# Attention and a four-expert MoE on one core: a small tile padded to 128 bytes, and three operand forms per pair of units written later

## Chip, cores and metric

One core of one Trainium2 chip. The metric is device time in microseconds (us), lower is better. The kernel before takes 1182.71 us, the median of three runs (1180.28 to 1183.48).

## The reference

The kernel computes attention with a local window and a few global keys, and feeds its output to four experts that are all applied to every token and mixed with given weights:

```python
def _attn_ref(q, k, v, n_global, n_local):     # 4 x 8 heads x 768 tokens x 64
    scores = scale * np.matmul(q, k.transpose(0, 1, 3, 2))
    ...
    scores = np.where(keep, scores + bias, -1000000000.0)
    ...
    return np.matmul(a, v).astype(np.float32)

def _moe_ref(x, domain_probs, w1, w2):         # x 3072 x 512, E = 4, F = 1024
    p = domain_probs / (domain_probs.sum(-1, keepdims=True) + 1e-09)
    for e in range(E):
        h = np.maximum(x @ w1[e], 0.0)
        out += p[:, e:e + 1] * (h @ w2[e])
    return out.astype(np.float32)
```

## The kernel before, in words

**Precision and fast multiplication.** Nearly all products of the experts run in fp32r. An operand is split into a high part (a rounded copy) and a low part (the operand less its high part), and three products, high by high, low by high and high by low, are summed in PSUM. Such a pair of parts is called a form here. The first matmul of an expert, x by w1, is a Strassen-Winograd product: x is cut into the blocks B11, B12, B21, B22 and their sums T1 to T4, w1 into A11, A12, A22 and sums S1 to S4, and seven block products (`product`, L850, 6 matmuls of 384 columns each) take the place of eight.

**Batches 0 and 1.** The attention of the first batch comes first (to about 63 us of the profile), then the expert layer of batches 0 and 1 with the attention of the later batches woven in. A unit is a batch, an expert and a group of 256 of the expert's 1024 inner columns: 16 units per batch. `first` (L872) makes the unit's hidden block and writes it, rectified, as tile `h` (pool `hp`, L1319); `second` (L937) multiplies it by w2: per unit 36 matmuls, `pm<-w2s,h`, with a piece of `h` of 128 x 128 as the stationary operand and 512 columns of `w2s` moving. Over the two batches these are 1152.

**Where the tiles lie.** Pools stand one behind the other in each partition of SBUF. Pool `fast` (L1275) holds the attention biases and `psumm` (L281), the 24 sums of the mixing weights, 96 bytes. It begins at a multiple of 64 bytes and ends, as built, at byte 130400, which is 32 past one. All pools opened behind it while it is open begin there or at whole multiples of 64 from it: the raw weights, the tiles of the attention (loaded q, k and v, their turned and split copies, the probabilities) and `h`. The forms of x, `w1s` and `w2s` lie ahead of it at multiples of 64. `early.close()` drops all of that; the pools of the turned batches (L1373) start afresh at a multiple of 64.

**Batches 2 and 3, the turned batches** (`turned_batch`, L982). Here the second matmul is a Strassen-Winograd product too. Two units make a pair j, eight pairs a batch. `small` (L1073) makes one unit's hidden block from seven products and leaves its four blocks, rectified and weighted, in the tiles hb["B11"], hb["B12"], hb["B21"] and hb["B22"], the even unit in the first half of each tile and the odd unit in the second. Once a pair has its blocks, `sums` (L995) makes T3, T1, T2 and T4 of them, and `form` (L988) writes the forms: ScalarE (ACT) the high part, a CAST, VectorE (DVE) or GpSimd (POOL) the low part, a subtraction. In the pair after it, `more` (L1183) calls `big` (L1049) seven times, between the products of `small`: n = 0 to 6 are A11 by B11, A12 by B21, S4 by B22, S3 by T3, S2 by T2, S1 by T1 and A22 by T4, of 12 matmuls each, `pq<-form,w2s` or `pq<-form,w2f`. n = 0 to 2 fall in the even unit, the rest in the odd one. A big product is added to an accumulator in SBUF by DVE; in the pair j = 1, where the accumulators are first written, ACT copies it there. The last pair of a batch is multiplied without turning (`multiply`, `pm<-w2s,form`: 12 matmuls of 512 columns per tile of 128 tokens, 144 in all), and the accumulators are turned back.

**What sets the order.** Each engine works through its own list. From the seventh step of batch 0 on a scheduler, at build time, sets the order on each engine, except that the instructions passed to `keep_in_program_order` keep theirs among each other and against what stands before them. The chain inside a unit: the matmuls of S2 by T2, S3 by T3 and A22 by T4 go on in the same accumulator (`pa`) as A11 by B11, and each has to wait until ACT has copied out what stood there: `u` (after S2 by T2) before S3 by T3 may start, `vv` (after S3 by T3) before A22 by T4. S4 by B22 goes on in the accumulator of S1 by T1 and waits until DVE has read that for block B22.

Names in the rows: hB_8000, hB_8001, hB_8002 and hB_8003 are hb["B11"], hb["B12"], hb["B21"] and hb["B22"]; hT_8004 is hb["T3"]; sumB_8005, sumB_8006 and sumB_8007 are the accumulators of big products 0, 1 and 2; `p`, `u` and `vv` are a unit's partial sums.

Of the kernel before, what the change touches and what calls it, by code (L numbers as in the profile page):

```python
# [9 lines left out]
F32 = mybir.dt.float32  # L10
# [8 lines left out]
P = 128  # L19
# [6 lines left out]
def f32(ap):  # L26
    return ap.bitcast(F32)
# [159 lines left out]
def attn_moe_kernel(ctx: ExitStack, tc, q, k, v, n_global, n_local, domain_probs, w1, w2, out):  # L187
# [19 lines left out]
    ve, ac, po, sy, te = (Ordered(tc, e) for e in (nc.vector, nc.scalar, nc.gpsimd, nc.sync, nc.tensor))  # L207
# [54 lines left out]
    NT = N // P  # L262
# [14 lines left out]
    def mixture():  # L277

        sy.dma_start(prob, domain_probs.rearrange("(t p) e -> p t e", p=P))
        yield  # L280
        psumm = fast.tile([P, NT, 1], F32, name="psumm")  # L281
        ve.reduce_sum(psumm, prob, axis=AX.X)
        ve.tensor_scalar_add(psumm, psumm, 1e-9)
        ve.reciprocal(psumm, psumm)
        for e in range(E):
            ve.tensor_mul(prob[:, :, e : e + 1], prob[:, :, e : e + 1], psumm)
# [485 lines left out]
    kept, waiting = {}, {}  # L772
# [209 lines left out]
    def turned_batch(b, L, hb, acc, raw):  # L982
# [2 lines left out]

        keeping = tc.keep_in_program_order

        def form(name, src, low):  # L988
            t = made[name] = L.form.tile([P, 2, 2, HALF], F32R, name="form")
            ac.copy(t[:, 0], src)  # L990
            ins = low.tensor_tensor(t[:, 1], src, f32(t[:, 0]), op=ALU.subtract)
            if low is po:
                keeping(ins)

        def sums():  # L995
            t3 = hb["T3"]
            ve.tensor_sub(t3, hb["B22"], hb["B12"])
            form("T3", t3, ve)
            ve.tensor_sub(hb["B12"], hb["B12"], hb["B11"])
            ve.tensor_add(hb["B11"], t3, hb["B11"])  # L1000
            form("T2", hb["B11"], ve)
            form("T1", hb["B12"], ve)
            ve.tensor_sub(hb["B21"], hb["B21"], hb["B11"])

        ORDER2 = (("A11", "B11"), ("A12", "B21"), ("S4", "B22"), ("S3", "T3"), ("S2", "T2"), ("S1", "T1"), ("A22", "T4"))

# [19 lines left out]
        def ask(j, n):  # L1026

            if j >= per // 2 - 1 or n in (0, 5):
                return
            e, g = divmod(j, NPR // 2)  # L1030
            names = {1: ("A11", "A12"), 2: ("S4",), 3: ("S3",), 4: ("S2",), 6: ("S1", "A22")}[n]
            if len(names) == 2:
                t = wp.tile([P, 2, 2, 2, 2 * P], F32R, name="w2s")
            else:
                t = L.w2f.tile([P, 1, 2, 2, 2 * P], F32R, name="w2f")
            for at, a in enumerate(names):
                to = w2f[(j, a)] = t[:, at]
                if a in value:
                    keeping(po.tensor_copy(to[:, :, 0], value[a]))
                    keeping(po.tensor_tensor(to[:, :, 1], value[a], f32(to[:, :, 0]), op=ALU.subtract))  # L1040
                else:
                    f, m = {"A11": (0, 0), "A12": (1, 0), "A22": (1, 1)}[a]
                    for u in range(2):
                        block = kept[(e, 2 * g + u, 2)][:, :, f, m * 2 * P : (m + 1) * 2 * P]
                        sy.dma_start(f32(to[:, u]), f32(block))
            if n == 6:
                ask_raw(j + 1)

        def big(j, n):  # L1049
            a, x = ORDER2[n]  # L1050
            pm = L.pq.tile([P, 2, 512], F32, name="pq")
            w, t = w2f[(j, a)], made[x]
            for m in range(2):
                at = 0
                for u in range(2):
                    for wi, xi in ((0, 0), (1, 0), (0, 1)):
                        te.matmul(
                            pm[:, m, :HALF], w[:, u, wi, m * P : (m + 1) * P], t[:, xi, u, :],
                            start=(at == 0), stop=(at == 5),
                        )  # L1060
                        at += 1
            if j == 0:
                ac.copy(acc[x], pm[:, :, :HALF])
            else:
                ve.tensor_add(acc[x], pm[:, :, :HALF], acc[x])
            if n == 0:
                form("T4", hb["B21"], ve)
            if j == per // 2 - 2:
                for to, other in {1: (("B21", "B11"),), 4: (("T2", "B11"), ("T3", "T2"))}.get(n, ()):
                    ve.tensor_add(acc[to], acc[to], acc[other])  # L1070
            ask(j + 1, n)

        def small(i, more, plain=None):  # L1073

            u = i % 2

            def out(name, f, c, src):
                if plain is None:
                    ve.scalar_tensor_tensor(
                        hb[name][:, u], src, 0.0, share[i][:, c * HALF : (c + 1) * HALF], op0=ALU.max, op1=ALU.mult  # L1080
                    )
                else:
                    if not plain:
                        for n in ((1, 0), (0, 1))[u]:
                            plain[n] = L.form.tile([P, 2, 2, HALF], F32R, name="form")
                    h = plain[f]
                    ac.activation(h[:, 0, c], src, AF.Relu)
                    ve.scalar_tensor_tensor(h[:, 1, c], src, 0.0, f32(h[:, 0, c]), op0=ALU.max, op1=ALU.subtract)
# [65 lines left out]
            h22 = hb["B22"][:, u]  # L1154
            ve.tensor_add(h22, pc[:, :HALF], u3)
            out("B22", 1, 1, h22)
            if u == 1 and plain is None:
                form("B22", hb["B22"], po)
            more()
# [13 lines left out]
        for j in range(per // 2):  # L1173
# [9 lines left out]
            def more():  # L1183
                if j > 0:
                    big(j - 1, at[0])
                else:
                    ask(0, at[0])
                at[0] += 1
# [6 lines left out]
            for i in (b * per + 2 * j, b * per + 2 * j + 1):  # L1195
                share[i] = pb
                plain = None
                if j == per // 2 - 1:
                    plain = final[i] = {}
                chores.append(load_w1(i + 2))  # L1200
                if j == per // 2 - 1:
                    chores.append(load_w2(i))
                for _ in small(i, more, plain):
                    work_chores()
                    yield
            if j < per // 2 - 1:
                sums()
# [67 lines left out]
    fast = early.enter_context(tc.tile_pool(name="fast", bufs=1))  # L1275
# [5 lines left out]
    with ExitStack() as start_stack:  # L1281
# [4 lines left out]
        for d, _ in enumerate(first_attention(A, bank)):  # L1286
# [19 lines left out]
            if d == 13:  # L1306
# [8 lines left out]
                last_forms(1, take, A)  # L1315
            work_chores()
        mix = mixture()
        next(mix)
    hp = early.enter_context(tc.tile_pool(name="hp", bufs=2))  # L1319
# [54 lines left out]
    hb = {n: L.hb.tile([P, 2, HALF], F32, name=f"h{n}") for n in ("B11", "B12", "B21", "B22", "T3")}  # L1374
# [39 lines left out]
```

## Time and profile before

| | us |
|---|---|
| median of three runs | 1182.71 |
| the profiled execution, whole | 1183.57 |
| its span, first to last instruction | 1181.8 |
| PE busy | 1155.9 (98%) |
| DVE busy | 841.2 (71%) |
| ACT busy | 527.8 (45%) |
| POOL busy | 469.0 (40%) |

The profiled execution is 0.86 us above the median, and 1.77 us of it lie outside the span. The busy time of PE counts a matmul up to its modelled end, so matmuls that follow each other overlap; how fast they follow is read from the starts in the timeline. PEld is the load of the stationary operand, which runs beside the matmul before it. An idle time is put down to what ended it.

### The profile page before, as it was taken

What the parts mean: (1) busy time and instruction counts of PE and PEld (TensorE: products, weight loads), DVE (VectorE), ACT (ScalarE), POOL (GpSimd) and SP (SyncE); (2) the same over time, 40 slices, a digit from 0 to 9 for tenths busy, and PEclk for the clock granted to TensorE, in tenths of its full rate; (3) what the DMA queues carried; (4) which work ended last, traced back from release to release, by engine and by line L of the source; (5) the groups of instructions that cost most, each with busy time, mean ns of one, the idle gap of its engine ahead of it and who ended that gap; (6) DMA issues with size and microseconds to landing.
All of it is one profiled execution on the core that took longest, in us unless ns stands there. A gap on an engine that the chain in (4) does not pass through costs nothing.

```text
span 1181.8 us, 19019 instructions
## 1 busy us (share of the span) xinstructions
PE 1155.9 (98%) x7101; PEld 1059.6 (90%) x7101; DVE 841.2 (71%) x1655; ACT 527.8 (45%) x1302; POOL 469.0 (40%) x437
## 2 busy tenths in 40 slices
PE   8989999999999999999999999999999999999998
PEld 6778888888888988888888899999999889999996
DVE  5976666676667766766666785787879566777784
ACT  5846666664655555445444314232234243222231
POOL 5666454545411000000000257666662376666620
PEclk9999999999999999999999999999999999999999
DMA  9578787767686675665655664666766556665532
GB/s 188 145 226 286 234 283 228 255 215 252 224 243 201 216 218 166 204 195 173 195 183 205 236 232 157 230 218 233 269 210 247 214 208 227 214 227 214 214 116 92
DMA packets 170116, 250.98 MB, mean 212 GB/s; under 512 B 108480, under 2 KB 144416, under 8 KB 157216
## 3 DMA queue, kind: packets, MB, share of 16 engines
q1 hardware_dynamic: 164976, 233.43, 60.7%
q0 software_dynamic: 4032, 14.68, 3.2%
q10 hardware_dynamic: 1008, 1.57, 0.4%
q8 instruction: 58, 0.95, 0.3%
q14 instruction: 42, 0.34, 0.1%
HBM read 194.04 MB, written 55.62 MB: 211 GB/s over the span
## 4 chain that ended last, share of the span: by engine, by line
PE 87%; DVE 8%; issue 1%; ACT 1%; DMA 1%; SPq 1%; POOL 0%; ACTq 0%; DVEq 0%
PE pm L42 62%; PE pq L42 14%; PE pt L42 7%; PE ps L42 4%; DVE hB L42 2%; DVE form L42 2%; DVE sumT L42 1%; DVE hT L42 1%; ACT form L42 1%; DVE pm L42 1%; SPq L42 1%; DVE sumB L42 0%; DMA first_k<-in_k_dram 0%; DMA raw<-in_moe_w_dram 0%; DMA raw_n<-in_n_local_dram 0%
## 5 line engine op out<-in xcount | busy, mean ns | idle before, releaser
L42 PE MATMUL pm<-xT,w1s 128*128 128x384 f32 x1536 | 303.8, 337 | 7.3 <-ACT vv L42 3.7
L42 PE MATMUL pm<-w2s,h 128*128 128x512 f32 x1152 | 286.2, 400 | 2.7 <-DVE h L42 2.7
L42 PEld LDWEIGHTS pm<-xT,w1s 128*128 128x128 f32 x1536 | 267.4, 188 | 10.5 <-ACT vv L42 4.4
L42 PEld LDWEIGHTS pm<-w2s,h 128*128 128x128 f32 x1152 | 212.6, 188 | 50.4 <-DVE h L42 3.5
L42 PE MATMUL pm<-xB,w1s 128*128 128x384 f32 x1152 | 229.4, 341 | 0.9 <-DVE hB L42 0.4
L42 PEld LDWEIGHTS pm<-xB,w1s 128*128 128x128 f32 x1152 | 203.5, 190 | 6.3 <-DVE hB L42 3.5
L42 DVE SCALAR_TENSOR_TENSOR acc<-pm,prob,acc 128x512 f32<-128x512 f32 x180 | 134.3, 749 | 75.8 <-PE pm L42 75.2
L42 POOL TENSOR_TENSOR xT<-x,xT 128x768 fp32r<-128x768 f32 x4 | 8.1, 2036 | 317.5 <-ACT xT L42 317.5
L42 PE MATMUL pq<-form,w2s 128*128 128x384 f32 x672 | 125.8, 334 | 0.0
L42 POOL TENSOR_TENSOR raw<-raw 128x512 f32<-128x512 f32 x56 | 74.7, 1334 | 113.8 <-DMA raw<-in_moe_w_dram 110.5
L42 PEld LDWEIGHTS pq<-form,w2s 128*128 128x128 f32 x672 | 117.3, 188 | 0.0
L42 ACT ACTIVATE pb<-pb,nmax 128x256 f32<-128x256 f32 (+1 forms) x192 | 92.5, 483 | 36.4 <-DVE nmax L42 35.7
L42 ACT CAST form<-hB 128x768 fp32r<-128x768 f32 x84 | 68.5, 836 | 85.5 <-DVE hB L42 85.5
L42 ACT COPY p<-pm 128x384 f32<-128x384 f32 x64 | 30.5, 477 | 147.9 <-PE pm L42 147.7
L42 PE MATMUL pq<-form,w2f 128*128 128x384 f32 x504 | 94.1, 334 | 0.0
L42 PEld LDWEIGHTS pq<-form,w2f 128*128 128x128 f32 x504 | 88.0, 188 | 0.0
L42 ACT ACTIVATE h<-pm 128x384 fp32r<-128x384 f32 x128 | 62.0, 488 | 54.2 <-DVE pm L42 49.7
L42 POOL TENSOR_TENSOR w2s<-raw,w2s 128x512 fp32r<-128x512 f32 x46 | 60.3, 1323 | 45.2 <-ACT w2s L42 43.9
L42 DVE SCALAR_TENSOR_TENSOR h<-pm,h 128x384 fp32r<-128x384 f32 x128 | 70.4, 552 | 7.7 <-ACT h L42 5.6
L42 DVE CUSTOM_DVE_ANT_0 pb<-ps,nbias 128x256 f32<-128x256 f32 (+1 forms) x144 | 50.3, 398 | 33.9 <-PE ps L42 27.7
L42 DVE TENSOR_TENSOR sumT<-pq,sumT 128x768 f32<-128x768 f32 x48 | 45.8, 953 | 36.9 <-PE pq L42 36.5
L42 ACT ACTIVATE pb<-pb,zsum 128x256 f32<-128x256 f32 (+1 forms) x144 | 62.5, 483 | 8.7 <-DVE zsum L42 8.3
(148 smaller groups left out, 1667.9 us busy)
## 6 DMA issues: line engine op xcount, KB each, us to landing
w1s<-kept SPq DMA_DIRECT2D x48, 1792.0 KB, 8.0
kept<-w1s SPq DMA_DIRECT2D x16, 1792.0 KB, 7.7
w2s<-kept SPq DMA_DIRECT2D x84, 256.0 KB, 5.0
w2s<-kept SPq DMA_DIRECT2D x20, 1024.0 KB, 4.9
raw<-in_moe_w_dram SPq DMA_DIRECT2D x32, 512.0 KB, 4.2
kept<-w2s SPq DMA_DIRECT2D x16, 1024.0 KB, 6.4
raw<-in_moe_w_dram POOLq DMA_DIRECT2D x28, 512.0 KB, 9.6
v<-in_v_dram SPq DMA_DIRECT2D x12, 384.0 KB, 5.8
```

The lines of the kernel that those rows point to most:

```text
L42: ins = fn(*args, **kwargs)
```

## The change

The sums of the mixing weights get a tile of 32 columns of which 24 are used, so that pool `fast` ends at byte 130432, a multiple of 64, and all that stands behind it moves up by 32 bytes: `h` from byte 142688 to 142720, for one. No tile of the turned batches moves.

In the turned batches T2 is added into T3's tile (once T3's form is made) and not into B11's. The forms of T2, T1 and T4 are no longer made in `sums` and at the first big product, but by a new function `rest_of_sums`, called in the even unit of the next pair behind the output of block B22. The three CASTs on ACT are kept in program order. The numbers of instructions on all engines stay the same.

```diff
-        psumm = fast.tile([P, NT, 1], F32, name="psumm")
+        psumm = fast.tile([P, 32, 1], F32, name="psumm")[:, :NT]
...
-        def form(name, src, low):
+        def form(name, src, low, kept=False):
             t = made[name] = L.form.tile([P, 2, 2, HALF], F32R, name="form")
-            ac.copy(t[:, 0], src)
+            ins = ac.copy(t[:, 0], src)
+            if kept:
+                keeping(ins)
             ins = low.tensor_tensor(t[:, 1], src, f32(t[:, 0]), op=ALU.subtract)
...
             form("T3", t3, ve)
             ve.tensor_sub(hb["B12"], hb["B12"], hb["B11"])
-            ve.tensor_add(hb["B11"], t3, hb["B11"])
-            form("T2", hb["B11"], ve)
-            form("T1", hb["B12"], ve)
-            ve.tensor_sub(hb["B21"], hb["B21"], hb["B11"])
+            ve.tensor_add(t3, t3, hb["B11"])
+            ve.tensor_sub(hb["B21"], hb["B21"], t3)
+
+        def rest_of_sums():
+            for name, src in (("T2", "T3"), ("T1", "B12"), ("T4", "B21")):
+                form(name, hb[src], ve, True)
...
-            if n == 0:
-                form("T4", hb["B21"], ve)
...
             out("B22", 1, 1, h22)
+            if u == 0:
+                rest_of_sums()
```

How this moves the instructions on ACT, in the pair j = 1 of batch 2 (the CASTs are the high parts of the forms, `u` and `vv` the copies that S3 by T3 and A22 by T4 wait for):

```order
 L42 CAST form<-hT_8004 128x768
 L42 COPY sumB_8005<-pq 128x768
 L42 COPY u<-pm 128x384
-L42 CAST form<-hB_8000 128x768
-L42 CAST form<-hB_8001 128x768
-L42 CAST form<-hB_8002 128x768
 L42 COPY sumB_8006<-pq 128x768
 L42 COPY vv<-pm 128x384
+L42 CAST form<-hT_8004 128x768
+L42 CAST form<-hB_8001 128x768
+L42 CAST form<-hB_8002 128x768
```

Three CASTs have moved from ahead of the copies of big product 1 and of `vv` to behind them. In the later pairs two of them stood ahead of `u` and one ahead of `vv`; there, too, all three now stand behind `vv`.

On DVE, in the pair j = 2 of batch 2, before (the rows that write `form` are the low parts of T2, T1 and T4; `hB_8002<-pm,share` is the output of block B21 of the even unit):

```order
L42 TENSOR_TENSOR hB_8002<-hB_8002,hB_8000 128x768
L42 TENSOR_TENSOR form<-hB_8000,form 128x768
L42 TENSOR_TENSOR form<-hB_8001,form 128x768
L42 TENSOR_TENSOR form<-hB_8002,form 128x768
L42 TENSOR_TENSOR pm<-pm,p_8473 128x384
L42 TENSOR_TENSOR sumB_8006<-pq,sumB_8006 128x768
L42 SCALAR_TENSOR_TENSOR hB_8000<-pm,share 128x384
L42 TENSOR_TENSOR hB_8003<-pm,vv 128x384
L42 TENSOR_TENSOR sumB_8007<-pq,sumB_8007 128x768
L42 SCALAR_TENSOR_TENSOR hB_8003<-hB_8003,share 128x384
L42 SCALAR_TENSOR_TENSOR hB_8002<-pm,share 128x384
```

and in the changed kernel:

```order
L42 TENSOR_TENSOR hB_8002<-hB_8002,hT_8004 128x768
L42 TENSOR_TENSOR pm<-pm,p_8467 128x384
L42 SCALAR_TENSOR_TENSOR hB_8000<-pm,share 128x384
L42 TENSOR_TENSOR sumB_8006<-pq,sumB_8006 128x768
L42 TENSOR_TENSOR hB_8003<-pm,vv 128x384
L42 SCALAR_TENSOR_TENSOR hB_8003<-hB_8003,share 128x384
L42 TENSOR_TENSOR form<-hT_8004,form 128x768
L42 TENSOR_TENSOR form<-hB_8001,form 128x768
L42 TENSOR_TENSOR form<-hB_8002,form 128x768
L42 TENSOR_TENSOR sumB_8007<-pq,sumB_8007 128x768
L42 SCALAR_TENSOR_TENSOR hB_8002<-pm,share 128x384
```

The outputs of blocks B11 and B22 now stand ahead of the three low parts, big product 2 and the output of B21 behind them. On PE only one thing moves, in the pair j = 1 of each turned batch: S4 by B22 of the even unit now stands ahead of A11 by B11 of the odd one, where it stood in its middle. Attention, the w2 preparation on POOL and all DMA issues on SP keep their order.

## Rows read from the trace of the kernel before

**Rows 1.** The page, chain that ended last: share of the span by engine.

```profile
PE 87%; DVE 8%; issue 1%; ACT 1%; DMA 1%; SPq 1%; POOL 0%; ACTq 0%; DVEq 0%
```

**Rows 2.** Windows: length, busy PE, PEld, DVE, ACT, POOL, granted clock, DMA, GB/s.

```profile
400.00:650.00 250.00, 250.00 (x1580) 220.91 (x1579) 165.76 (x397) 121.37 (x346) 0.00 (x0) 1.00 0.59 191
```

**Rows 3.** Groups of PE by form: names, shapes, count, busy us, mean ns.

```profile
L42 PE MATMUL pm<-w2s,h 128*128 128x512 f32 x1152 | 286.2, 400 | 2.7 <-DVE h L42 2.7
L42 PE MATMUL pm<-w2s,form 128*128 128x512 f32 x144 | 35.5, 397 | 0.0
L42 PE MATMUL pt<-ident,q 128*128 128x128 f32 x72 | 11.8, 272 | 0.0
L42 PE MATMUL pq<-ident,sumT 128*128 128x128 f32 x24 | 4.6, 275 | 0.9 <-DVE sumT L42 0.9
```

**Rows 4.** Groups of PEld by form.

```profile
L42 PEld LDWEIGHTS pm<-w2s,h 128*128 128x128 f32 x1152 | 212.6, 188 | 50.4 <-DVE h L42 3.5
L42 PEld LDWEIGHTS pm<-w2s,form 128*128 128x128 f32 x144 | 26.3, 188 | 5.4 <-DMA w2s<-kept 0.3
```

**Rows 5.** Timeline of PE, 24 matmuls with `h`: start us, us, what.

```profile
637.65 5.86 PE L42 MATMUL pm<-w2s,h 128*128 128x512 f32 x24
643.35 1.21 PE L42 MATMUL pm<-xB,w1s 128*128 128x384 f32 x6
```

**Rows 6.** Timeline of PE, 24 matmuls with `form`, in batches 2 and 3.

```profile
917.13 5.72 PE L42 MATMUL pm<-w2s,form 128*128 128x512 f32 x24
922.69 0.39 PE L42 MATMUL pq<-ident,sumB 128*128 128x128 f32 x2
...
1160.05 5.83 PE L42 MATMUL pm<-w2s,form 128*128 128x512 f32 x24
1165.71 0.38 PE L42 MATMUL pq<-ident,sumB 128*128 128x128 f32 x2
```

**Rows 7.** Timeline, batch 2, pair j = 1, even unit.

```profile
708.79 2.24 PE L42 MATMUL pq<-form,w2s 128*128 128x384 f32 x12
...
712.59 2.30 ACT L42 CAST form<-hB 128x768 fp32r<-128x768 f32 x3 [2.21 <-DVE hB L42]
...
713.82 2.68 DVE L42 TENSOR_TENSOR form<-hB,form 128x768 fp32r<-128x768 f32 x3
...
715.49 0.48 ACT L42 COPY vv<-pm 128x384 f32<-128x384 f32 x1
...
716.02 1.47 PE L42 MATMUL pm<-xT,w1s 128*128 128x384 f32 x6 [1.87 <-ACT vv L42]
...
721.02 1.22 PE L42 MATMUL pm<-xT,w1s 128*128 128x384 f32 x6
```

**Rows 8.** Windows: behind the wait of rows 7, and behind that of rows 11.

```profile
717.50:720.80 3.30, 3.30 (x11) 3.30 (x12) 1.95 (x4) 0.00 (x0) 2.38 (x2) 0.55 0.41 139
...
862.00:868.00 6.00, 5.83 (x32) 5.51 (x33) 6.00 (x10) 1.08 (x2) 1.73 (x2) 1.00 0.97 336
```

**Rows 9.** Timeline, batch 2, pair j = 2, the same stretch of the even unit.

```profile
741.84 2.24 PE L42 MATMUL pq<-form,w2s 128*128 128x384 f32 x12
...
742.34 2.69 DVE L42 TENSOR_TENSOR form<-hB,form 128x768 fp32r<-128x768 f32 x3
...
745.22 0.48 ACT L42 COPY vv<-pm 128x384 f32<-128x384 f32 x1 [1.82 <-PE pm L42]
...
746.74 0.54 DVE L42 TENSOR_TENSOR hB<-pm,vv 128x384 f32<-128x384 f32 x1
...
750.16 1.20 PE L42 MATMUL pm<-xT,w1s 128*128 128x384 f32 x6
```

**Rows 10.** Timeline of PE, batch 3, pair j = 1.

```profile
953.95 2.24 PE L42 MATMUL pq<-form,w2s 128*128 128x384 f32 x12
...
966.40 1.23 PE L42 MATMUL pm<-xT,w1s 128*128 128x384 f32 x6
```

**Rows 11.** Timeline of PE, batch 2, pair j = 6.

```profile
858.78 2.25 PE L42 MATMUL pq<-form,w2s 128*128 128x384 f32 x12
...
861.92 1.32 PE L42 MATMUL pm<-xT,w1s 128*128 128x384 f32 x6 [0.90 <-ACT u L42]
...
868.74 1.20 PE L42 MATMUL pm<-xT,w1s 128*128 128x384 f32 x6
```

## The prediction

> **What bounds the kernel now.** Read the chain that ended last first: PE makes 87% of it [rows 1], so the question of any edit is what PE waits for or how fast it goes. Then the windows by stage: from 400 to 650 us, with attention woven into the expert layer, PE is busy in all of 250.00 us while DVE has work for 165.76 and ACT for 121.37 [rows 2]. There PE sets the pace alone, and a matmul that follows its predecessor sooner shortens the span by as much. In the turned batches PE is as dense, but the timeline shows a few places where it stands, and the two parts of the change aim at one each of these: the padding at the rate of PE, the moved forms at its waits.
>
> **Part 1, the padding.** It adds and removes no instruction. What it touches on PE are the operands of the stages ahead of the turned batches, above all the 1152 stationary pieces of `h`, which lie 32 bytes past a multiple of 64 before and at one after. The trace holds a counterpart: the 144 matmuls with `form`, of the same shape, with the same kind of moving operand, whose stationary pieces lie at multiples of 64 already. Their load takes as long, 188 ns against 188 [rows 4], and their mean is 397 ns against 400 [rows 3]. But PE overlaps matmuls, so I go by starts. 24 with `h` take from 637.65 to 643.35, 5.70 us or 237.5 ns each [rows 5]; 24 with `form` take 5.56 and 5.66 us, 231.7 and 235.8 ns [rows 6]. Both kinds stand behind transposes, so both begin with the same change of shape. `h` is slower by 5.8 and 1.7 ns, 3.75 on the mean. The stretch of the `h` row is one with nothing on POOL [rows 2], so POOL doesn't explain it. I take 3.75 ns: 1152 x 3.75 = **4.3 us less**, all on the path by rows 2. Bounds from the same rows: 1152 x 1.7 = 2.0 and 1152 x 5.8 = 6.7; and nothing, if it is not the address that tells the two groups apart.
>
> The page "SBUF — State Buffer" of the Trainium skill, section Specifications (TRN2), gives SBUF lines of 16 bytes; 32 past a multiple of 64 begins such a line too, so by that page the padding buys nothing and the sum would be 1173.9. Rows 5 and 6 speak against it, with 3.75 ns per matmul.
>
> The other operands that move up by 32 bytes I cost at nothing. For transposes the trace excludes a gain: those of the loaded q, at 32 past, take 272 ns, those of the accumulators, aligned, 275 [rows 3]. For the scores and the products with v it has no aligned counterpart; the share that `h` shows (3.75 of 237.5, 1.6%) would be under 1 us on them, which goes into the range. That DVE, ACT or the DMAs gain or lose by the move no row shows, and in rows 2 they have room.
>
> **Part 2, the moved forms.** The count of instructions is the same, so only waits can change. I measure a stretch that is alike in every pair: from the start of big product 1 to S1 by T1 of the odd unit, 48 matmuls of 384 columns. In a pair without a wait, j = 2, it takes 750.16 - 741.84 = 8.32 us [rows 9], 0.173 each.
>
> - j = 1, batch 2: 721.02 - 708.79 = 12.23 us, 3.91 too long [rows 7]. A22 by T4 waits 1.87 us for the copy `vv`, which stands on ACT behind three CASTs and the copy of big product 1; the CASTs wait for T2 and T4 on DVE. The rest, 2.04 us, is the clock: behind the wait the granted clock is 0.55 of full [rows 8] in the mean, so for most of that stretch PE had the lower of its two levels, 1.2 GHz in place of 2.4. In the changed order the CASTs stand behind `vv`. The copy of big product 1 can start when that is done, 12 matmuls or 2.1 us after 708.79; `vv` follows S3 by T3 and is over by about 712.6, and A22 by T4 is not due before 714. Wait and clock loss go: 3.9 us.
> - j = 1, batch 3: 966.40 - 953.95 = 12.45 us, 4.13 too long [rows 10], the same place: 4.1 us.
> - j = 6, batch 2: 868.74 - 858.78 = 9.96 us, 1.64 too long [rows 11]. Here S3 by T3 waits 0.90 us for `u`, which stands behind the CASTs of T2 and T1; the rest is a second short wait and a change of shape, and the clock stayed at 1.00 [rows 8]. In the changed order only T3's CAST stands ahead of `u`: 1.6 us.
>
> Together **9.7 us less**. In the other pairs of the two batches this stretch holds smaller losses or none; I don't count them, and let the range take them.
>
> What the move puts later: the three CASTs and low parts. They now begin at `vv` of the even unit. In j = 2 that ends at 745.70 [rows 9]. DVE then does the sum and the output of B22 (two of 0.54) and the three low parts, 2.69, to about 749.5. Big products 4 to 6 read them, and big product 4 is due 30 matmuls behind S1 by T1 of the odd unit, at 750.16 + 30 x 0.173 = 755.4. So 6 us cover the forms, and without that cover each late us would be a us of PE. Behind the low parts DVE has big product 2's addition (another 0.9, as each of the low parts) and the output of B21, to 751.0. That output frees an accumulator bank of PE. As built, the odd unit's A12 by B21 takes that bank, due at 750.16 + 24 x 0.173 = 754.3: covered by 3.3 us. S1 by T1 of the odd unit takes the bank of the even unit's A12 by B21, which DVE now frees earlier. On ACT the kept CASTs delay the odd unit's copy `p`, but end by 745.70 + 2.6, before A11 by B11 of that unit does. On POOL and SP nothing moves. T3 of the next pair overwrites T2 only a whole unit later.
>
> **The sum.** 1183.57 (the profiled execution, 0.86 above the median of the runs) - 4.3 - 9.7 = **1169.6 us**. Against the median that is 1.1% less. A measurement of this kernel can tell about 0.3%, 3.5 us, from no change.
>
> **The rivals.**
>
> - *The padding buys nothing.* PE reads a stationary piece as fast from either address, and what tells `h` from `form` is something else, such as what runs beside it or how the 24 are grouped. For it: equal loads in rows 4, only 3 ns in rows 3. Against it: both `form` rows of rows 6 are below rows 5. Part 2 alone: 1183.57 - 9.7 = 1173.9. Chance 0.20. The Trainium skill's line of 16 bytes, above, would have it so.
> - *The waits come back elsewhere.* Something behind the new place of `vv` on ACT or of the low parts holds PE for as long as the old wait did, so that part 2 gives nothing and only the padding is left: 1183.57 - 4.3 = 1179.3. For it: ACT and DVE do as much work in the pair as before, and j = 1 has the slowest DVE. Against it: the covers worked out above. Chance 0.07.
> - *The change doesn't do what it says*: neither the addresses nor the old waits matter, 1183.6. Rows 7 name the wait, so 0.03.
> - *Slower: DVE frees a bank too late.* Mechanism: PE's next accumulator hangs on the output of B21, which now stands behind three low parts and an addition. It decides where PE wants that bank before DVE is through. If S1 by T1 of the odd unit hung on it, PE would stand 751.0 - 750.16 = 0.84 us in each of the 12 later pairs, 10.1 us. In j = 1, DVE reaches its low parts' place at 713.82 [rows 7]; two outputs and the sum of B22 (1.6), the low parts (2.68), an addition and the output of B21 (1.1) make 719.2 against 708.79 + 8.32 = 717.1, a wait of 2.1 us; a wait of that length costs another 2.04 of clock [rows 7, 8]: 8.3 in two batches. 18.4 lost, 9.7 won, with nothing from the padding 1183.57 + 8.7 = 1192.3. Against it: the bank that S1 by T1 takes is another one. Chance 0.06.
>
> **How the numbers follow.** Forecast, both parts: 0.64, with its own range from 1165 (padding 6.7, smaller waits gone too, a run at the median) to 1172.5 (padding 2.0, one of the short waits left, 0.6 of scatter). To hold 8 in 10 the range takes in the first rival and stops short of the third and fourth cases: 1164.5 to 1176.5. Faster by over 0.3%, below 1179.2: the forecast, the first rival and about half of the second, 0.87. Within 0.3%: the other half and the change that does nothing, 0.07. Slower: 0.06.
>
> **What would show it.** In the profile of the changed kernel: 24 matmuls with `h` in a row take about 5.6 us rather than 5.70, and their group's mean falls from 400 towards 397 ns; the 1152 of them, not other groups, hold the gain ahead of 690 us. In j = 1 of both turned batches PE has no wait on `vv`, the stretch takes about 8.3 us, and the granted clock stays at 1.00 behind it. No wait on `u` in j = 6. I am wrong on part 1 if the rows of `h` keep their 237 ns; on part 2 if PE waits for `pm` or `pq` banks, for `p`, or for a form of T2, T1 or T4 in the odd units.

## The result and the profile after

| | before | after |
|---|---|---|
| median, us | 1183.1 (1180.28 to 1184.6, 4 runs) | 1170.55 (1170.3 to 1172.45, 4 runs) |
| the profiled execution, us | 1183.57 | 1170.47 |
| its span | 1181.8 | 1168.7 |
| start to the first matmul with `h` | 83.02 | 81.14 |
| first to last matmul with `h` | 604.27 | 602.89 |
| from there to the end of the span | 494.51 | 484.66 |

Medians leave out one execution of the kernel with 48 columns (below), which took 1891.84 us at a granted clock of 0.557.

The changed kernel takes 0.99 of the time, 95% interval 0.9879 to 0.9922; 1169.6 us had been predicted. The gain of the two profiled executions, 13.1 us of span, lies in three places: 1.9 us ahead of the first matmul with `h`, 1.4 in the stage that the padding touches, 9.8 in the turned batches. The first had not been predicted, the second was predicted at 4.3, the third at 9.7.

**The turned batches.** The timeline of the changed kernel, batch 2, pair j = 1, even unit, answers to [rows 7] (start us, us, engine, what, and in brackets the idle time before it with what ended it):

```profile
705.46 2.24 PE L42 MATMUL pq<-form,w2s 128*128 128x384 f32 x12
...
707.74 0.80 ACT L42 COPY sumB<-pq 128x768 f32<-128x768 f32 x1 [0.64 <-PE pq L42]
...
708.78 0.48 ACT L42 COPY vv<-pm 128x384 f32<-128x384 f32 x1 [0.24 <-PE pm L42]
...
709.43 0.83 ACT L42 CAST form<-hT 128x768 fp32r<-128x768 f32 x1 [0.17 <-DVE hT L42]
...
710.17 1.57 ACT L42 CAST form<-hB 128x768 fp32r<-128x768 f32 x2
...
710.66 1.21 PE L42 MATMUL pm<-xT,w1s 128*128 128x384 f32 x6
...
713.04 1.82 DVE L42 TENSOR_TENSOR form<-hB,form 128x768 fp32r<-128x768 f32 x2
...
713.93 1.20 PE L42 MATMUL pm<-xT,w1s 128*128 128x384 f32 x6
```

The copy `vv` now waits only for its matmuls and is over at 709.26, 3.80 us behind the start of big product 1; predicted were 712.6 - 708.79 = 3.8. The three CASTs follow it. A22 by T4 starts at 710.66 without a wait, and S1 by T1 of the odd unit at 713.93: 8.47 us for the stretch instead of 12.23. In j = 1 of batch 3 and in j = 6 of batch 2 the stretch [rows 10, 11] now reads (timeline of PE of the changed kernel):

```profile
945.42 2.24 PE L42 MATMUL pq<-form,w2s 128*128 128x384 f32 x12
...
953.94 1.20 PE L42 MATMUL pm<-xT,w1s 128*128 128x384 f32 x6
```

```profile
851.21 2.24 PE L42 MATMUL pq<-form,w2s 128*128 128x384 f32 x12
...
859.53 1.20 PE L42 MATMUL pm<-xT,w1s 128*128 128x384 f32 x6
```

That is 8.52 us for 12.45 and 8.32 for 9.96. The three places together gave 3.76 + 3.93 + 1.64 = 9.33 us. The clock behind two of the places of the old waits [rows 8] is full now (windows of the changed kernel: stretch, length, busy PE, PEld, DVE, ACT, POOL, granted clock, DMA, GB/s):

```profile
709.00:717.00 8.00, 8.00 (x47) 7.83 (x46) 7.23 (x12) 3.74 (x6) 2.07 (x3) 1.00 0.95 314
854.00:862.00 8.00, 8.00 (x48) 8.00 (x48) 7.88 (x11) 3.16 (x5) 3.35 (x2) 1.00 1.01 357
```

What PE still waits for behind 684 us, by the view of its waits (total, times, longest, in us):

```profile
PE pq L42 <- DVE sumT L42: 0.9, 1, 0.9
PE pm L42 <- DVE hB L42: 0.5, 1, 0.5
```

The first stood there before, with 0.9 us [rows 3]. The second, at 887.21 in the last pair of batch 2, is a wait on the sum for block B22, which the profile before doesn't have at this place. That the later low parts cause it is not shown: with the padding alone, in the order of before, PE waits 0.43 us for the same sum in the same pair, at 891.56.

**The stage with `h`.** Rows of 24 and of 72 matmuls with `h`, timeline of PE, changed kernel; the row of 24 answers to [rows 5]:

```profile
634.60 5.82 PE L42 MATMUL pm<-w2s,h 128*128 128x512 f32 x24
640.25 1.22 PE L42 MATMUL pm<-xB,w1s 128*128 128x384 f32 x6
...
667.36 17.06 PE L42 MATMUL pm<-w2s,h 128*128 128x512 f32 x72 [0.30 <-DVE h L42]
684.26 1.21 PE L42 MATMUL pm<-xB,w1s 128*128 128x384 f32 x6
```

The same row of 72 in the kernel before:

```profile
670.56 17.13 PE L42 MATMUL pm<-w2s,h 128*128 128x512 f32 x72 [0.30 <-DVE h L42]
687.53 1.23 PE L42 MATMUL pm<-xB,w1s 128*128 128x384 f32 x6
```

24 take 5.65 us for 5.70 before, 72 take 16.90 for 16.97: 1 to 2 ns each. Two rows are a coarse measure, so from here on the spacing is the mean over the starts of all matmuls with `h` that follow another one within 300 ns, 1018 to 1024 in each trace: **234.1 ns before, 232.2 after**. The group's mean went from 400 to 399 ns [rows 3]:

```profile
L42 PE MATMUL pm<-w2s,h 128*128 128x512 f32 x1152 | 284.3, 399 | 2.7 <-DVE h L42 2.7
L42 PE MATMUL pm<-w2s,form 128*128 128x512 f32 x144 | 35.6, 397 | 0.0
```

**The start.** The first 20 us of the kernel before, and then of the changed one (windows):

```profile
0.00:20.00 20.00, 14.27 (x81) 11.21 (x82) 9.42 (x45) 10.10 (x36) 8.06 (x17) 0.93 0.96 184
```

```profile
0.00:20.00 20.00, 14.24 (x106) 11.20 (x106) 10.75 (x49) 10.89 (x39) 8.54 (x18) 1.00 0.98 190
```

The granted clock was 0.93 there and is 1.00 now. Whether that is the addresses or chance can't be read from two traces; the experiments tell.

### The profile page after: what moved, and what is told of

It reads as the page before. It is cut to its first block, busy times and chain, and to the rows that moved or that the text cites. A ratio compares the mean times of both kernels' runs of the same rounds, so it can differ in the third digit from the quotient of the medians.

```text
span 1168.7 us, 19036 instructions
## 1 busy us (share of the span) xinstructions
PE 1147.5 (98%) x7101; PEld 1055.6 (90%) x7101; DVE 869.1 (74%) x1655; ACT 528.0 (45%) x1302; POOL 481.1 (41%) x437
## 4 chain that ended last, share of the span: by engine, by line
PE 91%; DVE 4%; DMA 2%; ACT 1%; POOL 1%; SPq 0%; issue 0%; ACTq 0%; DVEq 0%
PE pm L42 63%; PE pq L42 16%; PE pt L42 7%; PE ps L42 4%; DVE sumT L42 1%; DMA w1s<-kept 1%; DVE hB L42 1%; SPq L42 0%; DMA w2s<-kept 0%; DVE form L42 0%; DVE pT L42 0%; DMA raw<-in_moe_w_dram 0%; DMA first_k<-in_k_dram 0%; DMA raw_n<-in_n_local_dram 0%; DVE pb L42 0%; POOL w2s L42 0%
## 5 line engine op out<-in xcount | busy, mean ns | idle before, releaser
L42 PE MATMUL pm<-xB,w1s 128*128 128x384 f32 x1152 | 226.4, 338 | 0.7 <-DVE hB L42 0.5
L42 PEld LDWEIGHTS pm<-xB,w1s 128*128 128x128 f32 x1152 | 201.0, 188 | 4.6 <-DVE hB L42 2.0
L42 POOL TENSOR_TENSOR raw<-raw 128x512 f32<-128x512 f32 x56 | 80.3, 1434 | 99.7 <-DMA raw<-in_moe_w_dram 96.4
L42 ACT CAST form<-hB 128x768 fp32r<-128x768 f32 x70 | 56.9, 836 | 61.5 <-DVE hB L42 61.5
L42 POOL TENSOR_TENSOR w2s<-raw,w2s 128x512 fp32r<-128x512 f32 x46 | 62.7, 1375 | 44.8 <-ACT w2s L42 43.5
L42 DVE TENSOR_TENSOR form<-hB,form 128x768 fp32r<-128x768 f32 x42 | 61.6, 1494 | 11.9 <-ACT form L42 11.7
L42 POOL TENSOR_TENSOR form<-hB,form 128x768 fp32r<-128x768 f32 x28 | 57.3, 2045 | 24.7 <-ACT form L42 24.7
```

Source lines behind the costliest of these rows:

```text
L42: ins = fn(*args, **kwargs)
```

## Experiments

Twelve runs were made, in three sets of four, each set beside the kernel before on its chip (medians of before 1182.77, 1183.75 and 1184.06 us).

### The padding alone (kernel before with)

```diff
-        psumm = fast.tile([P, NT, 1], F32, name="psumm")
+        psumm = fast.tile([P, 32, 1], F32, name="psumm")[:, :NT]
```

> The kernel before with the padded tile alone; the order on every engine is that of before. Theory (the addresses of TensorE's operands matter, by the 2 ns that the traces of before and after show between the starts of matmuls with h): 1152 x 2 ns = 2.3 us less at most, of which the stage with h showed 1.4 us; so 1180.8 to 1181.7 against 1183.1 of before, matmuls with h 232 ns apart instead of 234, and the wait on vv in the pair j = 1 still there at 1.9 us. Second question, the 1.9 us that the profile of after saved ahead of its first matmul with h (81.14 us against 83.02): if these too are addresses (transposes and scores of the first attention), the first h matmul starts near 81.1 here and the time is 1179 to 1180; if they are the granted clock of that one execution (1.00 against 0.93 in the first 20 us), it starts near 83 or anywhere between, whatever the addresses. Rival (the padding buys nothing): 1183.1, h matmuls 234 ns apart.

Measured: 1180.73 us, 0.9983 of before (0.9972 to 0.9994), 0.7 to 3.3 us less. Spacing 232.2 ns, stage 602.94 us. First matmul with `h` at 80.93. The waits on `vv` and on `u` are still there (waits of PE behind 684 us):

```profile
PE pm L42 <- ACT vv L42: 4.0, 2, 2.0
...
PE pm L42 <- DVE hB L42: 0.6, 2, 0.4
PE pm L42 <- ACT u L42: 0.5, 1, 0.5
```

But of the two waits on `vv` only the second cost clock (windows behind the first and the second):

```profile
713.00:716.60 3.60, 3.46 (x21) 3.15 (x20) 3.12 (x7) 0.38 (x2) 1.71 (x2) 1.00 0.88 278
957.10:960.70 3.60, 3.60 (x13) 3.35 (x12) 2.24 (x5) 0.10 (x1) 1.83 (x2) 0.53 0.65 232
```

The stretch from big product 1 on took 11.08 us in the first case, 12.24 in the second. Against the 8.47 of the changed kernel the first wait cost 2.6 us; 1.2 more came with the clock.

### The moved forms alone (changed kernel with)

```diff
-        psumm = fast.tile([P, 32, 1], F32, name="psumm")[:, :NT]
+        psumm = fast.tile([P, NT, 1], F32, name="psumm")
```

> The changed kernel with the small tile at its old 96 bytes, so that h and all else of the first two batches lie 32 bytes past a multiple of 64 again; the order on every engine is that of after. Theory: the moved forms alone, 9.85 us of the turned batches as the two traces show them, 1183.1 - 9.85 = 1173.3; h matmuls 234 ns apart again. The two edits touch different stages, so the gains of this run and of the padding alone should add up to the 12.5 us of both. If the 1.9 us of the start are addresses, the first h matmul starts near 83.0 here; if they are chance of the clock, at either value. Rival (the padding buys nothing, and all of the gain is the forms): 1170.6 as after, h matmuls 232 ns apart at the old address.

Measured: 1173.17 us, 0.9924 (0.991 to 0.9938), as expected. Spacing 234.1 ns again. The first matmul with `h` starts at 81.32 with nothing padded, so the 1.9 us of the start are not the addresses. The stage took 605.71 us, 1.44 more than before with the same addresses; the windows show why (the first 20 us, and behind the wait for `h` that ends at 81.32):

```profile
0.00:20.00 20.00, 14.37 (x102) 11.42 (x103) 10.62 (x47) 10.81 (x39) 7.40 (x16) 1.00 0.94 182
81.40:84.40 3.00, 3.00 (x7) 2.40 (x8) 1.84 (x5) 0.98 (x2) 2.59 (x7) 0.50 1.12 387
```

PE had the lower of its two levels, 1.2 GHz, behind a wait of 2.21 us. Behind the same wait the first profile of the changed kernel, 2.36 us long, kept 1.00.

### The forms behind block B11 instead of B22 (changed kernel with)

```diff
             out("B11", 0, 0, pd[:, :HALF])
+            if u == 0:
+                rest_of_sums()
...
             out("B22", 1, 1, h22)
-            if u == 0:
-                rest_of_sums()
```

> The changed kernel, but the forms of T2, T1 and T4 are called behind the output of block B11 of the even unit instead of B22: the CASTs then stand behind u on ACT, but ahead of the copy of big product 1 and of vv. Theory (the wait on vv, through the CASTs ahead of it, is what the move removed in j = 1): in j = 1 of both turned batches A22 by T4 waits on vv again, 1.9 to 2.4 us, with as much again lost to the lower clock behind it: 3.9 to 4.5 us each, 8 to 9 in the two, so 1178.4 to 1179.6; j = 6 keeps its gain, since u stands ahead of the CASTs. Rival (the wait itself costs, the clock behind it is chance): 4 to 5 us, 1174.5 to 1175.5. Second rival (the gain came from DVE's order, freeing banks sooner, not from ACT's): no wait on vv, 1170.6.

Measured: 1182.76 us, 1.0004 of before (0.9992 to 1.0017): **the whole gain of both parts is gone**, more than expected. The waits of PE behind 684 us:

```profile
PE pm L42 <- ACT vv L42: 3.9, 2, 2.1
PE pm L42 <- DVE hB L42: 1.6, 3, 1.1
```

The wait on `vv` is back in both places; the stretch takes 11.11 us and 12.09, and only behind the second did the clock fall (windows behind each):

```profile
714.90:718.50 3.60, 3.45 (x21) 3.13 (x20) 3.13 (x6) 0.39 (x2) 1.98 (x2) 1.00 0.75 244
958.70:962.50 3.80, 3.80 (x15) 3.47 (x14) 2.44 (x5) 0.24 (x1) 0.78 (x1) 0.55 0.72 262
```

Up to the last matmul the turned batches take 8.8 us longer than in the changed kernel's first profile, as expected in sum but not in its parts: 1.6 of PE's waits are on the sum for block B22 (hB), which no theory had. The longest, 1.06 us, stands in the pair j = 6 of batch 2, which was expected to keep its gain: there `u` is ahead of the CASTs, but on DVE the low parts are now ahead of that sum, and the stretch takes 9.65 us for the 8.32 of the changed kernel. Another 1.6 us went at the start, where the clock of this execution was 0.83, and 1.1 behind the last matmul, which stays unexplained.

### The CASTs not kept in program order (changed kernel with)

```diff
-                form(name, hb[src], ve, True)
+                form(name, hb[src], ve)
```

> The changed kernel without keeping the three CASTs in program order: the scheduler then puts them ahead of the copy of big product 1 and of vv in the pair j = 1, and ahead of vv in the later pairs, though they are called behind block B22. Theory (the place on ACT is what counts, and without the keeping the call behind B22 does not give it): the wait on vv is back in j = 1 of both turned batches, 1.8 to 2.2 us each, with the clock behind it lost in some executions, as in the run with the forms behind B11; 1178 to 1183. Rival (the place of the low parts on DVE is what helped): 1170.5 to 1172.

Measured: 1177.85 us, 0.9943 (0.9926 to 0.996), just under the range of the theory, beside 1172.15 of the changed kernel in the same set. In the pair j = 1 of batch 2 the CASTs stand ahead of the copy of big product 1 and of `vv` again (timeline), and PE waits behind 684 us as listed after it:

```profile
713.28 1.56 ACT L42 CAST form<-hB 128x768 fp32r<-128x768 f32 x2
...
714.74 0.79 ACT L42 COPY sumB<-pq 128x768 f32<-128x768 f32 x1
...
715.43 0.48 ACT L42 COPY vv<-pm 128x384 f32<-128x384 f32 x1
```


```profile
PE pm L42 <- ACT vv L42: 4.2, 2, 2.2
...
PE pm L42 <- DVE hB L42: 0.6, 1, 0.6
```

So the call behind block B22 alone doesn't move the CASTs on ACT; the keeping does. Both waits on `vv` (2.24 and 2.00 us) left the clock alone here (windows behind each):

```profile
716.40:720.00 3.60, 3.60 (x23) 3.60 (x22) 3.10 (x6) 0.69 (x2) 1.76 (x2) 1.00 0.83 260
958.90:962.50 3.60, 3.60 (x22) 3.60 (x22) 3.07 (x6) 0.67 (x2) 2.39 (x2) 1.00 0.87 283
```

### Where `h` lies, and where `form` lies

Four kernels move tiles by unused bytes and change nothing else. The tiles of the turned batches 32 bytes on:

```diff
+    skew = main.enter_context(tc.tile_pool(name="skew", bufs=1))
+    skewed = skew.tile([P, 8], F32, name="skewed")
     L = Pools(main, "late", dict(form=6, acc=1, w2f=3, hb=1, share=2, raw=1), dict(pq=2))
```

> The changed kernel with an unused tile of 32 bytes ahead of the pools of the turned batches, so that form, w2f and the other tiles of those batches that TensorE reads lie 32 bytes past a multiple of 64; nothing else moves. Address theory: the 144 matmuls with form go from 229 ns apart to 231 to 234, 0.3 to 0.7 us; the 1176 matmuls of 384 columns that read form as the moving or w2f as the other operand, 173.3 ns apart now, lose up to 2 ns each, 2.4 us: 1170.9 to 1173.6. Rival (the address is nothing, h differs from form by what runs beside it): spacing unchanged, 1170.6.

`h` alone 32 bytes on:

```diff
+    skew = early.enter_context(tc.tile_pool(name="skew", bufs=1))
+    skewed = skew.tile([P, 8], F32, name="skewed")
     hp = early.enter_context(tc.tile_pool(name="hp", bufs=2))
+    skew2 = early.enter_context(tc.tile_pool(name="skew2", bufs=1))
+    skewed2 = skew2.tile([P, 8], F32, name="skewed2")
```

> The changed kernel with 32 unused bytes ahead of the pool of h and 32 behind it: h alone lies 32 bytes past a multiple of 64 again, all other tiles of the first two batches at multiples of 64. Theory (the stationary operand h is what the padding helped): matmuls with h 234 ns apart as before, against 232.2 in the four profiles with h aligned; the stage from the first to the last of them takes 1.4 to 1.9 us longer than the 602.9 us of the aligned kernels, 604.3 to 604.8, and the time is 1172.0 to 1172.5 without a clock loss (up to 1173.2, the time of the kernel with nothing padded, if the clock falls behind the wait at 81 us as it did there). Rival (it is the tiles of the attention that gained): 232 ns, 602.9 us, 1170.6.

48 columns in the small tile, which moves `h` and all behind it by 64 bytes:

```diff
-        psumm = fast.tile([P, 32, 1], F32, name="psumm")[:, :NT]
+        psumm = fast.tile([P, 48, 1], F32, name="psumm")[:, :NT]
```

> The changed kernel with a small tile of 48 columns in place of 32, so that h and all else of the first two batches lie 64 bytes past a multiple of 128 (a multiple of 64 still; in the changed kernel h is at a multiple of 128). Theory (a multiple of 64 is enough): h matmuls 232.2 ns apart, stage 602.9 us, 1170.6. Rival (a multiple of 128 is what counts, 64 past it costs as 32 past did): 234 ns, 604.3 us, 1172 to 1173.2.

`h` and the tiles behind it 128 bytes on, those of the turned batches 64:

```diff
+    skew = early.enter_context(tc.tile_pool(name="skew", bufs=1))
+    skewed = skew.tile([P, 32], F32, name="skewed")
     hp = early.enter_context(tc.tile_pool(name="hp", bufs=2))
...
+    late_skew = main.enter_context(tc.tile_pool(name="late_skew", bufs=1))
+    late_skewed = late_skew.tile([P, 16], F32, name="late_skewed")
     L = Pools(main, "late", dict(form=6, acc=1, w2f=3, hb=1, share=2, raw=1), dict(pq=2))
```

> The changed kernel with 128 unused bytes ahead of the pool of h, and 64 ahead of the pools of the turned batches: h lies at a multiple of 128 as in the changed kernel, but 128 bytes on; form and w2f lie 64 bytes past a multiple of 128 instead of at one. So far, by the place of h within 128 bytes: 0 gave 232.2 ns, 32 gave 233.6, 64 gave 229.3, 96 (the kernel before) 234.1; form at 0 gave 229.2 and at 32 gave 232.8. Theory (the place within 128 bytes decides): h 232.2 ns again and its stage 602.9 us; form at 64 as fast as at 0 or faster, 226 to 229.5; 1170.5. Rival (a longer period, the place within 256 bytes or more): h moves to another value, 229 or 234 ns, the stage by minus 3.3 or plus 1.4 us; then form may move too.

Measured, with the addresses of the built kernels taken by multiples of 256 bytes, and `w2s`, the moving operand, always at one:

| kernel | `h`, bytes past a multiple of 256 | spacing, ns | first to last matmul with `h`, us | time, us (ratio to before) |
|---|---|---|---|---|
| `h` 128 bytes on | 0 | 228.5 | 598.68 | 1169.88 (0.9875; 0.9859 to 0.9892) |
| before | 96 | 234.1 | 604.27 | |
| changed kernel | 128 | 232.2 | 602.89 | 1170.55 (0.99) |
| `h` alone 32 on | 160 | 233.6 | 604.13 | 1171.93 (0.9906; 0.9887 to 0.9925) |
| 48 columns | 192 | 229.3 | 599.63 | 1167.24 (0.9877; 0.9849 to 0.9906) |

For `form`, the stationary operand of the 144 matmuls at the end of the batches (124 to 128 spacings a trace): 229.2 ns at 0 in the changed kernel, and 229.2 to 230.0 over the twelve traces with `form` there; 232.8 at 32 (1173.36 us; 0.9927, 0.991 to 0.9943), 233.3 at 64 (the row with `h` 128 bytes on, which pays for this too). The row of 72 shows it by itself; first `h` alone 32 on, then 48 columns, then `h` 128 bytes on:

```profile
668.35 17.06 PE L42 MATMUL pm<-w2s,h 128*128 128x512 f32 x72 [0.30 <-DVE h L42]
685.24 1.21 PE L42 MATMUL pm<-xB,w1s 128*128 128x384 f32 x6
```

```profile
664.38 16.76 PE L42 MATMUL pm<-w2s,h 128*128 128x512 f32 x72 [0.30 <-DVE h L42]
680.98 1.23 PE L42 MATMUL pm<-xB,w1s 128*128 128x384 f32 x6
```

```profile
665.35 16.60 PE L42 MATMUL pm<-w2s,h 128*128 128x512 f32 x72 [0.30 <-DVE h L42]
681.79 1.23 PE L42 MATMUL pm<-xB,w1s 128*128 128x384 f32 x6
```

16.89, 16.60 and 16.44 us for the same 72 matmuls. Three things follow.

- The address of the stationary operand is the cause. Between "`h` alone 32 on" and "48 columns" every tile that TensorE reads in this stage lies alike but `h`, and the spacing differs by 4.3 ns, the stage by 4.5 us. The attention's tiles, which lie differently in the other kernels, are not needed to explain the rest: against the changed kernel, 1152 times the difference in spacing gives the difference of the stage within 0.8 us in every row.
- Neither "a multiple of 64" nor "a place within 128 bytes" is the rule, so both theories put on record fell: `h` at two multiples of 128 gave 232.2 and 228.5, at one multiple of 64 between them 229.3. The rival put on record with the last kernel, a longer period, is what is left. A place within 256 bytes fits all eight values, those of `h` and of `form` together, but with one value or two per place that is a description and not a proof.
- Where the moving operand lay made no loss at the two places tried: the 672 matmuls `pq<-form,w2s`, whose moving `form` went from 0 to 32 bytes, kept 173.3 ns, and took 173.0 at 64. `pq<-form,w2f`, whose stationary `w2f` moved with it, went from 173.3 to 175.8 at both.

### Two waits less, and the changed kernel again

The late addition, in the last pair:

```diff
-                for to, other in {1: (("B21", "B11"),), 4: (("T2", "B11"), ("T3", "T2"))}.get(n, ()):
+                for to, other in {3: (("B21", "B11"),), 4: (("T2", "B11"), ("T3", "T2"))}.get(n, ()):
```

> The changed kernel with the addition of accumulator B11 into accumulator B21 of the last pair moved from big product 1 to big product 3, two products later. In the profile of after it stands on DVE at 885.73 us for 0.9 us, ahead of the sum for block B22 at 886.60, for which PE waits 0.47 us at 887.21 and loses 0.64 with the step to the next matmul. Theory: that wait goes, 0.6 to 0.75 us, 1169.8 to 1170.0. Rival (the addition is then late for the last matmuls' transposes, whose wait at 908.07 us grows by the 0.9 us of the addition): 0 to 0.3 us slower than after, 1170.6 to 1170.9.

The late turn, on top of it:

```diff
-        for mul, back in ((0, ()), (1, (0, 1)), (2, (2, 3)), (3, (4,)), (4, (5,)), (5, ())):
+        backs = ((0, ()), (1, (0, 1)), (2, (2, 3)), (3, (4,)), (4, (5,)), (5, ()))
+        if b < LAST:
+            backs = ((0, ()), (1, ()), (2, (0, 1)), (3, (2, 3)), (4, (4,)), (5, (5,)))
+        for mul, back in backs:
```

> The kernel with the late addition, and in batch 2 the accumulators turned back one tile of 128 tokens later (the first transposes behind 36 matmuls with form instead of 12), so that PE has work while DVE ends the last sums; batch 3 is unchanged. In the profile of after the transposes wait 0.94 us at 908.07 and lose 1.1. Theory: this wait goes too, 1.0 to 1.1 us, together with the late addition 1.7 us under after: 1168.8 to 1169.0. Rival (the accumulators are given out later, so that batch 3 starts with fewer free PSUM banks or buffers): a new wait of 0.5 to 2 us between 915 and 925 us, 1169.5 to 1172.

The changed kernel once more, without an edit:

> The changed kernel itself, on the same chip as the other three of this set, so that small differences can be told. Theory (without the waits on vv only two places are left where the clock is chance, the first 20 us and the stretch behind the wait at 81 us): most runs within 0.5 us of 1170.5, single ones 1.4 to 2 us above, none above 1174.5; the kernel before 1180 to 1186 beside it. Rival (the narrow scatter of the first four runs was luck): a spread of 5 us as before has.

The late addition, the late turn and the small tile of 48 columns together:

> The kernel with the small tile of 48 columns (h 64 bytes past a multiple of 128), the late addition and the late turning back. The trace of the run with 48 columns had matmuls with h 229.3 ns apart and its stage at 599.6 us, 3.3 under after; the run with the late turn had the turned batches at 477.4 us, 1.4 under after. Theory (the two gains lie in different stages and add): 4.7 us under the changed kernel of this set, 1165.8 if that is at 1170.5. Rival (the gain of the late turn was eaten by a later wait, as the medians of those runs showed no gain): 3.3 us, 1167.2.

Measured: late addition 1171.96 us (0.9905; 0.9884 to 0.9926) and late turn 1170.66 (0.9895; 0.9874 to 0.9916), both above what their theories had; the changed kernel again 1172.15 (1169.77 to 1172.49; 0.9891, 0.9875 to 0.9908), all that with 48 columns 1167.57 (0.9865; 0.9848 to 0.9881).

From the start of the last matmul with `h` to the end of the last matmul the traces read 478.81 us (changed kernel), 479.69 (again), 478.16 (late addition), 477.42 (late turn), 477.63 (both). In the last pair of batch 2 the wait on the sum for block B22 is 0.11 us with the late addition, 0.25 with the late turn on top and 0.16 with both edits and 48 columns, against 0.47 and 0.96 in the two profiles of the changed kernel: shorter, but not gone. The late turn removed the wait on the last sums. In the medians these 0.7 and 1.4 us can't be told from the scatter. With `h` at 192 and both edits the time is 4.6 us under the changed kernel of its set, as expected (4.7); the intervals of the two ratios still overlap by 0.0006. By its ratio it is the best version that ran, but 48 columns alone (0.9877) can't be told from it.

The narrow scatter of the first runs did not hold: three of four runs of the changed kernel were at 1171.9 to 1172.5. The profile among them (1172.49) had a full clock in the first 20 us, but lost it behind the wait at 81 us (window 81.20 to 84.80):

```profile
81.20:84.80 3.60, 3.60 (x10) 2.75 (x11) 2.54 (x6) 0.98 (x2) 2.84 (x7) 0.53 1.03 380
```

## Why the prediction was right, and where it was not

**In all.** 1169.6 was predicted, 1170.55 and, in the last set, 1172.15 came: inside the range, by the likeliest case. One term was nevertheless too large by 2.9 us, and in the two profiled executions chance at the start gave 1.9 of them back: that the total came within 1 us is in part luck.

**Part 2 was right, in place, mechanism and size.** 9.7 us were predicted and 9.8 came; 9.33 of them at the three places named. For the waits on `vv` the order on ACT is shown to be the cause by the two kernels that put the CASTs back ahead of `vv`: in both, the waits of 2 us return in j = 1 of both batches. For `u` in j = 6 no kernel put the CASTs back ahead of it, so there the cause rests on the profiles before and after; and in the kernel with the forms behind B11, where `u` is clear but the low parts stand ahead of the sum for block B22 on DVE, PE waited 1.06 us at that place, so the place on ACT alone was not enough there. None of the covers failed: no wait on the output of B21, on `p` or on a form of T2, T1 or T4 appears. The wait on the sum for block B22 in the last pair (0.64 us lost with the step behind it) was in no term; it is there with the padding alone too, so it is no price of the move that these runs show.

**One thing in part 2 was put too firmly: the clock.** The step read "wait and clock loss go: 3.9 us", as if a wait of 1.87 us always cost 2 us of clock. Over the four profiles that have the wait (before, padding alone, forms behind B11, not kept) it stood eight times, 1.83 to 2.24 us long, and the clock fell behind four of them. Without it the stretch took 10.6 to 11.1 us, with it 12.1 to 12.5, against 8.5 in the changed kernel. So each wait cost 2.1 to 2.6 us by itself and, where the clock fell, another 1.3 on the mean (12.25 against 10.92); the profile predicted from had lost it both times. The Trainium skill, "TensorE: Matmul & The Clock Gate", Part 1, says that the window in which activity is watched runs freely and does not start anew with the kernel, so that the point at which the clock rises varies. Four falls in eight waits are compatible with that, but no run here shows such a window.

**Part 1 was mis-sized.** The term was 1152 x 3.75 ns = 4.3 us. The spacing fell by 1.9 ns, half of the 3.75 and worth 2.2 us, just above the lower bound of 2.0; the stage itself fell by 1.4 us, below it, and the medians with the padding alone by 2.0 (0.7 to 3.3). The failing step is the counterpart: `form` was taken as what `h` would be "at a multiple of 64". The difference between the two was real, 234.1 against 229.5 ns over all matmuls of before, 4.6 ns. But `form` lies at multiples of 256, and the padding took `h` from 96 to 128 past one. At 0 past one `h` does reach 228.5 ns, and the stage is 5.6 us shorter than before: with another 128 bytes of padding the gain would have been between the term, 4.3, and its upper bound, 6.7. The other operands that move were put at nothing, and that held: by the same measure, between 90 and 684 us, the scores (`ps<-ks,qs`) are 63.5 ns apart before and 63.7 after, the transposes of the probabilities (`pt<-ident,pb`) 116.1 and 116.0, the products with v (`pt<-pT,v`) 41.4 and 41.4. The rival that the padding buys nothing is excluded for `h` by the same table. The Trainium skill's lines of 16 bytes in SBUF ("SBUF — State Buffer", Specifications (TRN2)) don't tell any of these addresses apart, since all begin such a line; the measured 228.5 to 234.1 ns decide.

**The 1.9 us of the start were chance.** In 14 profiles the first matmul with `h` starts at 80.9 to 81.5 us in the nine with a granted clock of 1.00 in the first 20 us, and at 82.6 to 83.0 in the five with 0.83 to 0.95; padded and unpadded kernels are in both groups. Seven of the profiles are of kernels that are alike up to there, in the order on each compute engine and in every address; four of these are in the first group, three in the second. What sets the clock in these 20 us is open. Of the 13.1 us between the two profiled executions, 1.9 are thus no gain of the change.

## What to carry to other kernels

Read a wait's price in two parts, the wait itself, which returned here in every profile with the CASTs ahead, and the clock behind it, which did not: one profile shows one throw. When a fast group of matmuls serves as the counterpart of a slow one, write down the full address of both operands, not the residue that the edit happens to name; a stationary operand at another multiple of 32 bytes was worth up to 5.6 ns per matmul of 512 columns here. An instruction that belongs behind another on a shared engine has to be held there: the place of the call alone did not do it.

## What was not expected of the hardware

- The place of the stationary operand changed the spacing of matmuls of 512 columns from 228.5 to 234.1 ns, while the load itself stayed at 188 to 189 ns. What in the load or in the reads beside it costs the nanoseconds is open, and so is whether the place counts by itself or against that of the moving operand, which was never moved for these.
- With the pools of the turned batches 32 bytes on, the matmuls `pm<-xT,w1s` in those batches, none of whose operands moved, went from 173.4 to 174.9 ns apart. This stays unexplained.
- Behind the wait of 2.2 to 2.4 us at 81 us the clock fell in 5 of 14 profiles, at 1.4 to 1.6 us each, and those waits were 2.18 to 2.22 us long, while those of the other nine, 2.20 to 2.40, left it alone: the longer wait isn't the one that costs. That a kernel scatters less with two of three such places gone is not shown: eight runs of the changed kernel spread over 2.7 us, seven of the kernel before over 4.9 in one set and 2.1 in another.
